# Rewriting an attention plus mixer kernel: full-array matmuls, activations kept in SBUF, 512-token MLP groups interleaved with attention, and crossbar transposes

## The chip, the cores and the metric

The kernel runs on one core of a Trainium2 chip. The metric is the device time of one launch in microseconds (us). Several executions were timed for each kernel; the text quotes medians. A run more than 1.5% above the fastest of its kernel counts as slow and stays out of the ratios.

Engine names in the profile: PE is TensorE (matmuls), PEld is the weight load of TensorE (it overlaps PE: in the kernel before the two are busy 442.4 and 746.2 us of a span of 883.4), DVE is VectorE, ACT is ScalarE, POOL is GpSimd, SP is SyncE. A "q" after a name (SPq) is the sequencer or queue of that engine. PEclk is the TensorE clock that was granted, as a share of full speed.

## The reference

The problem has 8 batches of 576 tokens. Attention has 8 heads of 64 channels, a band of 32 tokens to each side, and 8 global tokens. A mixer block follows it.

```python
# attention, per batch and head (q, k, v: 576 x 64)
scores = q @ k.T / sqrt(64)
mask   = |i - j| <= 32  or  i is global  or  j is global
attn   = softmax(where(mask, scores, -1e9));  x[:, head] = attn @ v
# mixer, per batch (x: 576 x 512)
tok = w_tok @ (alpha1 * x + beta1);     u = x + lam * tok          # token mix
ch  = relu((alpha2 * u + beta2) @ w_ch1) @ w_ch2                   # channel MLP, 512 -> 2048 -> 512
out = u + lam * ch
```

## The kernel before

The kernel before has two stages in sequence, and DRAM tiles between them. In the first stage each head loads q, k and v, transposes q and k on TensorE, and computes scores with operands of 64 rows. The product with V opens each of five output tiles with an 8-row matmul (the eight global keys) and adds two 128-row matmuls to it (one in the last tile).

```python
# stage 1, per batch and head (cut)
for c in range(NT):
    nc.tensor.transpose(out=trq[:, c, :], in_=qn16[:, c, :], identity=identb)        # L369
nc.vector.tensor_copy(out=QT, in_=trq)                                               # QT, KT: 64 rows
...
nc.tensor.matmul(out=scps[...], lhsT=KTf[:, c : c + P], rhs=QT[:, t, :], start=True, stop=True)           # L385, 64 rows
...
for t in range(NT):                                                                  # partB
    nc.tensor.matmul(out=pvps[...], lhsT=st["pgc"][:, gsl], rhs=st["vg_ext"], start=True, stop=False)     # L424, 8 rows
    for ci, bi in enumerate(tbis):
        nc.tensor.matmul(out=pvps[...], lhsT=PT[:, bi * P : (bi + 1) * P], rhs=rhs, start=False, ...)     # L429, 128 rows
...
nc.sync.dma_start(out=pxd.rearrange("(t p) f -> p t f", p=P), in_=prev["xstg"])      # x to DRAM
nc.gpsimd.indirect_dma_start(out=pxd, ..., in_=prev["xg"], compute_op=ALU.add)       # global rows added in DRAM
```

The token mix of batch b-1 is emitted in pieces among the heads of batch b. It reads x back from DRAM, and stores u to DRAM. The second stage reads u, transposes it on TensorE in fp32, and runs the MLP over 576 tokens in two halves of 288.

```python
# stage 2, per batch (cut)
nc.sync.dma_start(out=U, in_=u_dram[b])
for t in range(NT):
    for cc in range(4):
        nc.tensor.transpose(out=utps[:, cc, 0:tsz], in_=U[...], identity=ident[...])         # L504, fp32
    nc.vector.tensor_copy(out=UT[...], in_=utps[:, :, 0:tsz])                                # L505
for ec in range(16):
    for nn in range(2):                                                                      # 2 x 288 tokens
        ... 4 matmuls hps (L513), 1 Relu on ScalarE (L516)
for t in range(NT):                                                                          # 4 x 128 + 64 tokens
    ... 16 matmuls chps of 512 columns (L522), add U, store
```

The softmax here doesn't subtract the row's maximum and nothing guards it: scores larger than these inputs give would overflow.

## Time and profile before

| | before |
|---|---|
| time, median of the first 3 runs | 873.48 us (868.25 to 884.87) |
| TensorE recorded busy | 746.2 us, 84% |
| TensorE's share of the chain that ended last | 76% |
| set-up, with TensorE mostly idle | about 60 us |
| attention and token mix | about 468 us, 58 us per batch |
| hand-over through DRAM | about 30 us |
| channel MLP | about 330 us, 41 us per batch |

The profiled execution is the longest of the first three runs (span 883.4 us, device time 884.87), 1.9% above the fastest. The differences that the profile is read for are far larger than that. The lines below are from the page of the kernel before: busy time of each engine with its share of the span and its number of instructions, busy tenths and clock tenths in 40 equal slices (22 us each), and the chain that ended last.

```profile
PE 746.2 (84%) x5044; PEld 442.4 (50%) x5091; DVE 340.5 (39%) x865; ACT 326.1 (37%) x641; POOL 155.8 (18%) x295
...
PE   0158999998989989989999872989898989898998
...
PEclk9999999855656555556555575998998999899989
...
PE 76%; DVE 11%; DMA 7%; issue 3%; ACT 1%; SPq 0%; POOL 0%; POOLq 0%; DVEq 0%
```

TensorE is recorded as busy nearly everywhere after the set-up, and the chain lies mostly on it. The clock row shows that the busy share is not the whole story: between slice 9 and slice 24 the granted clock is about half, although TensorE is recorded as busy at 80% or more up to slice 23.

The next view is the table by windows for the kernel before. Its columns are the window, its length, then for each engine the busy us and the number of instructions, then the granted clock, the DMA share, and GB/s.

```profile
0.00:60.00 60.00, 11.91 (x98) 6.74 (x99) 29.93 (x103) 0.00 (x0) 1.37 (x7) 1.00 0.50 182
...
176.00:234.00 58.00, 52.99 (x395) 30.95 (x396) 32.01 (x86) 24.65 (x48) 19.39 (x36) 0.56 0.54 156
526.00:556.00 30.00, 9.17 (x42) 5.34 (x43) 11.25 (x12) 0.00 (x0) 1.46 (x1) 0.60 0.51 194
556.00:597.00 41.00, 38.13 (x228) 22.98 (x230) 7.38 (x12) 15.87 (x32) 0.00 (x0) 0.97 0.24 90
```

The four windows are the set-up, one batch of attention, the hand-over, and one batch of the MLP. The stages follow each other, so each has its own limit. TensorE has only 9 us of work in the 30 us of the hand-over.

Two stretches of TensorE's timeline show where its busy time goes. Columns: start, length, engine and line, operation with output and inputs, rows*columns of the array, shape, and number of matmuls in the group. A gap before the group and what ended it stand in square brackets.

```profile
103.50 0.23 PE L424 MATMUL pvps<-vg_ext,pgc 8*128 8x65 f16 x1
103.67 0.29 PE L429 MATMUL pvps<-vext,PT 128*128 128x65 f16 x2
103.89 0.23 PE L424 MATMUL pvps<-vg_ext,pgc 8*128 8x65 f16 x1
...
401.44 0.20 PE L424 MATMUL pvps<-vg_ext,pgc 8*128 8x65 f16 x1
401.58 0.23 PE L429 MATMUL pvps<-vext,PT 128*128 128x65 f16 x2
401.74 0.20 PE L424 MATMUL pvps<-vg_ext,pgc 8*128 8x65 f16 x1
...
619.24 14.11 PE L522 MATMUL chps<-W_199,HT 128*128 128x512 bf16 x63
...
634.72 0.66 PE L504 MATMUL utps<-ident,U 128*128 128x128 f32 x4 [0.90 <-DVE UT L505]
```

A tile of three 65-column matmuls, one with 8 rows and two with 128, takes 0.39 us at 103 us and 0.30 us at 401 us (start to start). A record is longer than the distance to the next start (0.23 us against about 0.06 us for two such matmuls of one mode), so lengths overlap; the distance between starts is what counts. In the MLP 63 matmuls of 512 columns take 14.1 us, so 0.22 us each. The MLP then stops for the fp32 transposes, with gaps of 0.8 to 0.9 us.

### The profile page before, as it was taken

The numbers are of one execution on the slowest core, as the hardware profiler recorded it, in microseconds if no ns is written. First come the engines' busy times: TensorE is split into PE (matmuls) and PEld (weight loads), VectorE is DVE, ScalarE is ACT, GpSimd is POOL, SyncE is SP. The second block draws the span as 40 slices with busy tenths as digits, with TensorE's granted clock in tenths as the row PEclk, the third lists the DMA queues.
The fourth block names the chain that finished last, engine by engine and source line by source line (L and its number), as shares of the span: only waits on it lengthen the run. The fifth ranks groups of instructions, "written<-read, shape, count | busy, mean of one in ns | idle before, by whom it ended". The sixth has DMA issues, their size and how long they took to land.

```text
span 883.4 us, 13205 instructions
## 1 busy us (share of the span) xinstructions
PE 746.2 (84%) x5044; PEld 442.4 (50%) x5091; DVE 340.5 (39%) x865; ACT 326.1 (37%) x641; POOL 155.8 (18%) x295
## 2 busy tenths in 40 slices
PE   0158999998989989989999872989898989898998
PEld 0026665564554654645545531646464645555564
DVE  2654446547465474474544734120202020211111
ACT  0005554443443433434524320616060624334251
POOL 0025433233242332313413200000000000000000
PEclk9999999855656555556555575998998999899989
DMA  4926464473652754636526425120302020202101
GB/s 121 374 53 161 115 179 131 146 205 77 204 162 75 216 159 141 191 85 198 160 72 191 130 108 192 61 95 18 114 13 102 15 100 36 78 36 78 49 6 54
DMA packets 116807, 103.81 MB, mean 118 GB/s; under 512 B 90504, under 2 KB 91032, under 8 KB 114184
## 3 DMA queue, kind: packets, MB, share of 16 engines
q1 hardware_dynamic: 108536, 83.57, 30.5%
q0 software_dynamic: 8208, 19.40, 7.2%
q8 instruction: 40, 0.66, 0.3%
q14 instruction: 23, 0.19, 0.1%
HBM read 72.23 MB, written 30.71 MB: 117 GB/s over the span
## 4 chain that ended last, share of the span: by engine, by line
PE 76%; DVE 11%; DMA 7%; issue 3%; ACT 1%; SPq 0%; POOL 0%; POOLq 0%; DVEq 0%
PE chps L522 15%; PE hps L513 15%; PE tkps L292 9%; PE scps L385 7%; PE pvps L429 7%; PE pvps L424 5%; PE trq L369 5%; PE scps L375 3%; PE pvps L406 3%; DMA w2raw<-in_moe_w_ch_dram 3%; DVE XL L282 2%; PE smp L438 2%; PE utps L504 2%; DVE X L278 2%; DVE UT L505 2%
## 5 line engine op out<-in xcount | busy, mean ns | idle before, releaser
L516 ACT ACTIVATE HT<-hps,bias1T 128x288 bf16<-128x288 f32 x256 | 127.2, 501 | 213.1 <-PE hps L513 212.6
L513 PE MATMUL hps<-UT,W_192 128*128 128x288 bf16 x1024 | 154.7, 293 | 1.6
L522 PE MATMUL chps<-W_199,HT 128*128 128x512 bf16 (+1 forms) x608 | 152.7, 381 | 2.9 <-ACT HT L516 1.3
L513 PEld LDWEIGHTS <-W_192 128*128 128x128 bf16 x1024 | 102.0, 100 | 48.3 <-issue 20.2
L526 DVE TENSOR_TENSOR ob<-chps,U 128x512 f32<-128x512 f32 (+1 forms) x40 | 27.6, 690 | 249.5 <-PE chps L522 249.5
L396 ACT ACTIVATE PT<-scps 128x1192 f16<-128x1192 f32 x64 | 74.5, 1164 | 109.3 <-PE scps L388 102.1
L292 PE MATMUL tkps<-XL,wtT 128*128 128x512 bf16 (+3 forms) x185 | 80.3, 555 | 19.4 <-DVE XL L282 15.6
L522 PEld LDWEIGHTS <-HT 128*128 128x128 bf16 (+1 forms) x640 | 62.4, 100 | 64.1 <-issue 3.4
L385 PE MATMUL scps<-QT,KT 64*128 64x128 bf16 x576 | 78.5, 283 | 7.6 <-DVE KT L376 7.6
L446 DVE COPY xstg<-pvps 128x320 f32<-128x320 f32 x64 | 31.4, 491 | 121.7 <-PE pvps L429 121.7
L424 PE MATMUL pvps<-vg_ext,pgc 8*128 8x65 f16 x320 | 72.0, 225 | 2.3 <-DVE vg_ext L411 2.0
L429 PE MATMUL pvps<-voext,PT 128*128 128x65 f16 x448 | 69.3, 234 | 0.0
L415 ACT ACTIVATE pgc<-pvps 8x640 f16<-8x640 f32 x64 | 44.3, 692 | 62.9 <-PE pvps L406 62.9
L306 POOL DMA_DIRECT2D vn<-in_v_dram x63 | 58.3, 926 | 49.5 <-ACT vext L357 38.7
L385 PEld LDWEIGHTS <-KT 64*128 64x128 bf16 x576 | 53.3, 125 | 21.8 <-DVE KT L376 11.4
L504 PE MATMUL utps<-ident,U 128*128 128x128 f32 (+1 forms) x160 | 29.6, 309 | 37.5 <-DVE X L278 19.5
L388 PE MATMUL scps<-qgT,KT 64*128 64x8 bf16 x320 | 61.1, 207 | 0.0
L351 POOL DMA_DIRECT2D vo<-in_v_dram x64 | 53.2, 831 | 11.7 <-ACT voext L360 9.3
L429 PEld LDWEIGHTS <-PT 128*128 128x128 f16 x576 | 39.9, 109 | 22.7 <-issue 3.8
L421 DVE TENSOR_TENSOR PT<-PT,mask 128x1192 f16<-128x1192 f16 x64 | 49.1, 768 | 2.6 <-ACT PT L396 2.2
L424 PEld LDWEIGHTS <-pgc 8*128 8x128 f16 x320 | 31.2, 98 | 33.4 <-issue 6.6
L292 PEld LDWEIGHTS <-wtT 128*128 128x128 bf16 (+3 forms) x200 | 21.4, 125 | 47.2 <-issue 42.6
(486 smaller groups left out, 834.4 us busy)
## 6 DMA issues: line engine op xcount, KB each, us to landing
qn<-in_q_dram SPq DMA_DIRECT2D x63, 160.0 KB, 2.6
kn<-in_k_dram SPq DMA_DIRECT2D x63, 160.0 KB, 3.3
vn<-in_v_dram POOLq DMA_DIRECT2D x63, 160.0 KB, 3.5
vo<-in_v_dram POOLq DMA_DIRECT2D x64, 128.0 KB, 3.3
out_dram<-ob SPq DMA_DIRECT2D x32, 256.0 KB, 2.0
w1raw<-in_moe_w_ch_dram SPq DMA_DIRECT2D x1, 4096.0 KB
w2raw<-in_moe_w_ch_dram SPq DMA_DIRECT2D x1, 4096.0 KB
xdram_60<-xstg SPq DMA_DIRECT2D x1, 1300.0 KB, 6.1
```

The costliest lines, as they stand in the source:

```text
L292: nc.tensor.matmul(out=tkps[0:tsz, :], lhsT=wtT[0:ssz, sc, t * P : t * P + tsz], rhs=st["XL"][0:ssz, sc, :], start=(sc == 0), stop=(sc == 4),)
L306: eng.dma_start(out=dst, in_=src_flat[bh * S : bh * S + SPAD, :].rearrange("(c p) d -> p c d", p=P))
L351: nc.gpsimd.dma_start(out=vo, in_=vf[bh * S + 64 : bh * S + S, :].rearrange("(c p) d -> p c d", p=P))
L385: nc.tensor.matmul(out=scps[:, bi * P : (bi + 1) * P], lhsT=KTf[:, c : c + P], rhs=QT[:, t, :], start=True, stop=True)
L388: nc.tensor.matmul(out=scps[:, GR_OFF + 8 * si : GR_OFF + 8 * si + 8], lhsT=KTf[:, c : c + P], rhs=g["qgT"][:, 8 * h : 8 * h + 8], start=True,
L396: nc.scalar.activation(out=PT, in_=scps[:, 0:SCORE_F], func=AF.Exp, bias=0.0, scale=0.125)
L421: nc.vector.tensor_tensor(out=PT, in0=PT, in1=mask, op=ALU.mult)
L424: nc.tensor.matmul(out=pvps[:, t * PV_T : t * PV_T + PV_T], lhsT=st["pgc"][:, gsl], rhs=st["vg_ext"], start=True, stop=False)
L429: nc.tensor.matmul(out=pvps[:, t * PV_T : t * PV_T + PV_T], lhsT=PT[:, bi * P : (bi + 1) * P], rhs=rhs, start=False, stop=(ci == len(tbis) ...
L513: nc.tensor.matmul(out=hps, lhsT=W1[:, cc, ec * P : (ec + 1) * P], rhs=UT[:, cc, tsl], start=(cc == 0), stop=(cc == 3))
L516: nc.scalar.activation(out=HT[:, ec, tsl], in_=hps, func=AF.Relu, bias=bias1T[:, ec : ec + 1], scale=1.0)
L522: nc.tensor.matmul(out=chps[0:tsz, :], lhsT=HT[:, ec, t * P : t * P + tsz], rhs=W2[:, ec, :], start=(ec == 0), stop=(ec == 15))
```

## The change

The intent is that TensorE should run one array mode, with large matmuls back to back, and that attention should hide among the matmuls of the MLP.

- Every matmul uses 128 rows and 128 columns, one small transpose in the set-up apart. Two heads share the 128 rows; q is laid out with zeros in the other head's rows. The 8 global keys of all heads share one 128-row operand (G and RG).
- x and u stay in SBUF. The DRAM round trips are gone.
- The MLP runs over nine flat groups of 512 tokens. The last 64 tokens of two batches make one shared tile ("S").
- q, k, u and w_tok are transposed by DMA through the crossbar (`dma_start_transpose`: the data are transposed on their way), apart from q and k of batch 0 and the gathered global rows.
- Attention and token mix of batch g+1 are placed between the 128 matmuls of group g, by a fixed program order; below this is called the weave.
- W2 is loaded and scaled during group 0.

```diff
 # cut to the core
-for c in range(NT):
-    nc.tensor.transpose(out=trq[:, c, :], in_=qn16[:, c, :], identity=identb)
+def xbar_k(b, c):
+    nc.sync.dma_start_transpose(out=KT[b % 2][:, :, 32 + c * P : 32 + (c + 1) * P], in_=Kb[:, c, :])
 ...
-nc.tensor.matmul(out=pvps[...], lhsT=st["pgc"][:, gsl], rhs=st["vg_ext"], start=True, stop=False)
+def pv_mms(b, hp, i, o):
+    mm(o, G[:, gs], RG[hp % 2], True, False)
+    for a in range(2):
+        mm(oa, pt[:, a, c0 : c0 + P], Ve[par][:, i, 2 * hp + a, :], False, i == 4)
 ...
-nc.sync.dma_start(out=u_dram[bb], in_=st["U"].rearrange("p t c -> p (t c)"))
+def finish_u(t, ps):
+    nc.vector.tensor_tensor(out=x, in0=ps, in1=x, op=ALU.add)
+    nc.gpsimd.tensor_tensor(out=ub, in0=x, in1=A2, op=ALU.mult)
+    nc.sync.dma_start_transpose(out=UT[g % 2][:, :, 128 * j : 128 * j + 128], in_=ub)
 ...
+def attention(b):          # scores s, products with V w, per pair of heads
+    ...
+            a += [s[0], w[0], s[1], w[1], w[2], s[2], w[3], w[4]]
+        if i < HP:
+            a.append(gq_pv(b, i))           # global queries; makes RG
 ...
+for w, f in token_mix(0):
+    f()
+...
+for f in xbars(1):         # ten q/k transposes of batch 1
+    f()
+for hp in range(HP):
+    qpad(hp)               # VectorE: QT -> QP, zero-padded
+gcols(1)                   # VectorE: KGP
+for g in range(9):
+    base = mlp(g)          # 64 matmuls of W1, 64 of W2, 512 columns each
+    if g == 0:
+        slots[0] += [lambda: w2_load(0), lambda: w2_load(1)]
+        ... w2_scale(blk) at slot 8 + 7 * blk
+    if nb < NB:            # nb = g + 2
+        timed(prefetch(nb), slots, 2, 60)
+        timed(xbars(nb), slots, 60, 100)
+        timed([... qpad ..., gcols(nb)], slots, 116, 127)
+    parts = [(attention(g + 1), 2, 90), (token_mix(g + 1), 94, 114)] if g + 1 < NB else []
+    weave(items, parts)
```

## The prediction

> **What bounds it now.** The chain of waits lies 76% on TensorE, 11% on VectorE, 7% on DMA. The table by windows shows serial stages:
> - set-up, about 60 us, TensorE busy 12 us;
> - attention plus token mixing, 60 to 528 us: a 58 us period per batch, TensorE recorded busy 53 of it, granted clock 0.50 to 0.59 from 176 us on;
> - after a 30 us hand-over, the channel MLP, about 41 us per batch at clock 0.93 to 1.0.
>
> Timeline: in MLP runs the 512-wide matmuls start 0.22 us apart, the 288-wide 0.122 us, so 80+128 need 33 us; the rest is mostly fp32 transposes of U (0.8 us gaps). In attention two same-mode 65-wide matmuls start 0.06 us apart, but a tile of one 8-row and two 128-row matmuls takes 0.30 to 0.39 us, not 0.18: up to 0.1 us per change of array mode. [...]
>
> **What the change does.** It removes all 64-row and 8-row modes, PE transposes of q, k and U after batch 0, the DRAM round trips of x and u, and ragged 576-token MLPs. Per batch, attention needs 36 score matmuls, 20 global, 92 PV (each near 0.062 us), 8 of 288 columns (0.122) and 25 token-mix of 512 (0.218): estimate 2.3+1.2+5.7+1.0+5.4 = 15.7 us. An MLP group of 128 matmuls of 512 columns: 27.9 us, nine of them.
>
> Estimate of the whole:
> - set-up and attention of batch 0, not overlapped (DMA, ACT and VectorE hops, token mixing, q/k crossbar transposes ahead of group 0): 70 us;
> - group 0, with W2 loaded and scaled underneath: 51 us;
> - groups 1 to 6: 43.6 us of matmuls each plus 3 us of stalls: 280 us;
> - groups 7, 8: 56 us; last stores 3 us.
>
> Sum 460 us. Other engines per 46 us group, from traced durations (ACT about 0.29 us + 0.73 ns per column; VectorE 0.69 us per 512 fp32 columns): ACT 19 us, VectorE 22 us; GpSimd an estimated 30 us (15 loads near 1 us, multiplies). So TensorE stays the bound, nearly all of the removed time was on the critical path, and attention under dense matmuls should keep the clock near 1.
>
> **Predicted: 460 us, 8 in 10 between 425 and 515. Faster 0.97, same 0.015, slower 0.015.**
>
> **What would show the steps.**
> - MLP matmuls 0.218 us apart, attention's 0.06 to 0.07, no mode gaps between; TensorE above 85% busy in groups.
> - Group 0 starting at 60 to 80 us; 44 to 48 us for groups 1 to 6, 28 us for 7 and 8.
> - Granted clock 0.9 or more from group 0 on.
> - Busy: ACT 150 to 190 us, VectorE 190 to 240 us.
>
> **What would make it wrong.**
> - Crossbar transposes: 14 or 15 of 128 KB per group on one in-order queue; the trace before has none. [...] at 1 to 1.5 us each they fit, at 4 us they would set the group (60 us) and give 560 us.
> - GpSimd: casting loads and multiplies in one queue; at 1.5 times my estimate it sets the group.
> - The clock falling to half in mixed groups: over 100 us.
> - A longer serial start: W1 and W_tok share the DMA with batches 0 and 1.
> - Tighter dependence of score, exp, mask, PV: 1 us per head pair is 28 us.

The 1 to 1.5 us and the 4 us for a crossbar transpose were estimates, since the trace before has none. So was the part of the multiplies in the 30 us for GpSimd; for the loads the trace before shows 0.83 to 0.98 us each.

## The result and the profile after

| | before | after |
|---|---|---|
| time, median of 4 runs | 879.17 us (868.25 to 892.9) | 496.74 us (495.06 to 497.37) |
| ratio of fast runs | | 0.567 (95% interval 0.563 to 0.5711) |
| HBM read / written | 72.23 / 30.71 MB | 39.38 / 9.44 MB |
| TensorE busy, matmuls | 746.2 us, x5044 | 387.7 us, x2727 |
| mean granted clock | 0.786 | 0.952 |

Ratios in this document are the mean time of one kernel's fast runs over that of the other's of the same rounds, so they are not quite the ratio of the medians that are quoted. The 0.567 comes out when the profiled run of the kernel before (884.87 us) is counted as fast; without it the ratio is 0.570. The outputs are right.

These are the lines of the page of the kernel after, in the order of those of before. A slice is 12.3 us here.

```profile
PE 387.7 (79%) x2727; PEld 204.8 (42%) x2727; DVE 241.4 (49%) x697; ACT 155.7 (32%) x275; POOL 218.8 (44%) x270
...
PE   0336640657897889978998898899889888999995
...
PEclk9998585687999999999999999999999999999999
...
PE 44%; DVE 23%; DMA 10%; issue 8%; SPq 5%; ACT 5%; POOL 3%; POOLq 0%; DVEq 0%; ACTq 0%
```

From slice 11 on the clock is full (1.00 from 123.3 us to the end), and until the last slice TensorE is busy for at least seven tenths. The first ten slices are different: TensorE is busy for 0 to 7 tenths, and the clock falls to half (0.50 between 50 and 60 us and between 74.3 and 89.1 us). VectorE's share of the chain has risen from 11% to 23%.

The same table by windows for the kernel after: set-up, group 0, group 1, group 2, group 7 and group 8. The borders are the starts of the first W1 matmul of each group, read from the timeline.

```profile
0.00:74.30 74.30, 30.20 (x298) 21.63 (x299) 44.45 (x133) 16.68 (x33) 41.14 (x54) 0.88 1.16 155
74.30:150.40 76.10, 49.69 (x317) 25.03 (x318) 41.44 (x108) 17.01 (x30) 32.41 (x40) 0.80 0.85 131
150.40:195.00 44.60, 40.70 (x304) 21.59 (x304) 22.85 (x69) 16.66 (x30) 22.89 (x30) 1.00 1.07 117
195.00:244.50 49.50, 43.65 (x317) 22.89 (x318) 27.04 (x82) 16.68 (x30) 30.02 (x36) 1.00 1.00 109
432.80:460.50 27.70, 27.70 (x130) 12.57 (x129) 2.77 (x4) 10.99 (x16) 0.00 (x0) 1.00 0.15 51
460.50:493.30 32.80, 27.74 (x129) 12.38 (x127) 3.46 (x5) 10.99 (x16) 0.00 (x0) 1.00 0.12 40
```

Groups start at 74.3, 150.4, 195.0, 244.5, 289.9, 339.3, 384.9, 432.8 and 460.5 us. Groups 1 to 6 take 282.5 us together, 44.6 to 49.5 us each; the longer ones carry six token-mix tiles and the shorter ones four. In groups 1 and 2 TensorE idles 4 to 6 us. Group 0 takes 76 us for the same matmuls, and TensorE is idle for 26 of them. Its busy time is longer too: 49.7 us against 43.7 us in group 2, which has as many matmuls on record (317). At the clock of 0.80 the matmuls themselves cost about 6 us more, an estimate from these two lines.

The timeline of TensorE in the kernel after, inside group 0 at a clock of 1.00 (97 to 100 us), answers to the two stretches of before:

```profile
98.43 0.22 PE L119 MATMUL bank<-RG,G 128*128 128x130 f16 x1
98.49 0.19 PE L119 MATMUL bank<-Ve,PT 128*128 128x65 f16 x1
98.52 0.19 PE L119 MATMUL bank<-Vo,PT 128*128 128x65 f16 x1
98.55 0.19 PE L119 MATMUL bank<-Ve,PT 128*128 128x65 f16 x1
98.58 0.20 PE L119 MATMUL bank<-Vo,PT 128*128 128x65 f16 x1
98.61 0.81 PE L119 MATMUL bank<-UT,W 128*128 128x512 bf16 x3
```

A tile of V products for two heads, five matmuls, now takes 0.18 us from start to start; before, the tiles of two heads took 0.60 to 0.78 us. The 65-column matmuls start 0.03 us apart. No gap separates attention from the MLP.

The waits of TensorE in the kernel after (total us, times, longest us):

```profile
PE bank L119 <- DVE RG L310: 32.7, 25, 3.3
PE bank L119 <- DVE KGP L222: 17.9, 6, 13.8
PE bank L576 <- DVE UT L570: 17.5, 3, 10.9
PE bank L119 <- DMA UT<-UB: 7.6, 2, 7.4
```

RG and KGP are operands for the global tokens, UT is u transposed (in the set-up, at L570 and L576, the same tile holds q and k of batch 0).

The second line holds one wait of 13.8 us. It stands at the start of group 0, and the queue of SyncE shows where it comes from:

```profile
64.24 6.33 SPq L403 DMA_TRANSPOSE UT<-UB  x4
70.61 1.26 SPq L208 DMA_TRANSPOSE KT<-Kb  x1
71.92 1.26 SPq L211 DMA_TRANSPOSE QT<-Qb  x1
...
82.57 1.22 SPq L211 DMA_TRANSPOSE QT<-Qb  x1
83.97 0.46 SPq L204 DMA_DIRECT2D Vo<-Ve  x1
```

The ten crossbar transposes of q and k of batch 1 are queued behind the four transposes of u, which come out of the token mix of batch 0. Each holds the queue for about 1.25 us, against 0.46 us for a plain copy. They end at 84 us. VectorE then copies QT into QP (85.17 us) and KGP after that, and the first attention matmul of group 0 starts at 89.11 us.

### The profile page after: what moved, and what is told of

It reads as the page before. It is cut to its first block, busy times and chain, and to the rows that moved or that the text cites. A ratio compares the mean times of both kernels' runs of the same rounds, so it can differ in the third digit from the quotient of the medians.

```text
span 493.3 us, 7444 instructions
## 1 busy us (share of the span) xinstructions
PE 387.7 (79%) x2727; PEld 204.8 (42%) x2727; DVE 241.4 (49%) x697; ACT 155.7 (32%) x275; POOL 218.8 (44%) x270
## 3 DMA queue, kind: packets, MB, share of 16 engines
HBM read 39.38 MB, written 9.44 MB: 99 GB/s over the span
## 4 chain that ended last, share of the span: by engine, by line
PE 44%; DVE 23%; DMA 10%; issue 8%; SPq 5%; ACT 5%; POOL 3%; POOLq 0%; DVEq 0%; ACTq 0%
PE bank L119 43%; DVE PT L292 4%; DVE QP L216 4%; ACT E L280 3%; DVE PGQ L287 3%; DMA UT<-UB 3%; DMA KG<-in_k_dram,hidx 2%; DVE RG L310 2%; SPq L208 2%; SPq L211 2%; DVE XR L338 2%; DVE RGt L309 2%; DMA XR<-in_moe_w_ch_dram 1%; DVE SR L338 1%; POOL UB L401 1%
## 5 line engine op out<-in xcount | busy, mean ns | idle before, releaser
L119 PE MATMUL bank<-UT,W 128*128 128x512 bf16 x576 | 160.7, 387 | 9.2 <-DMA UT<-UB 7.6
L119 PE MATMUL bank<-W,HT 128*128 128x512 bf16 x576 | 142.5, 379 | 0.0
L470 ACT ACTIVATE HT<-bank,bias 128x512 bf16<-128x512 f32 x144 | 98.9, 687 | 85.3 <-PE bank L119 82.5
L119 PEld LDWEIGHTS <-HT 128*128 128x128 bf16 x576 | 52.0, 98 | 50.6
L401 POOL TENSOR_TENSOR UB<-XR,A 128x512 bf16<-128x512 f32 x32 | 40.5, 1267 | 58.9 <-DMA UT<-UB 25.8
L119 PEld LDWEIGHTS <-W 128*128 128x128 bf16 x640 | 50.8, 99 | 35.9 <-issue 11.0
L119 PE MATMUL bank<-RG,G 128*128 128x130 f16 x160 | 36.0, 226 | 32.7 <-DVE RG L310 32.7
L280 ACT ACTIVATE E<-bank 128x416 f16<-128x416 f32 (+1 forms) x96 | 48.0, 511 | 40.5 <-PE bank L119 40.3
L483 DVE TENSOR_TENSOR XR<-bank,XR 128x512 f32<-128x512 f32 x32 | 21.9, 685 | 54.9 <-PE bank L119 54.9
L119 PE MATMUL bank<-XL,wtT 128*128 128x512 bf16 x180 | 44.9, 379 | 0.8 <-ACT wt4o L688 0.8
L119 PE MATMUL bank<-Ve,PT 128*128 128x65 f16 x320 | 40.6, 199 | 0.0
L398 DVE TENSOR_TENSOR XR<-bank,XR 128x512 f32<-128x512 f32 x32 | 22.1, 691 | 36.1 <-PE bank L119 36.1
L216 DVE COPY QP<-QT 64x576 bf16<-64x576 bf16 x56 | 25.0, 446 | 18.7 <-DMA QT<-Qb 18.1
```

The lines of the kernel that those rows point to most:

```text
L119: nc.tensor.matmul(out=o, lhsT=l, rhs=r, start=st, stop=sp, skip_group_check=True)
L216: nc.vector.tensor_copy(out=QP[r, hp, a, :, 0:64], in_=QT[r, hp, 0:S].rearrange("p (t j) -> p t j", j=64))
L280: nc.scalar.activation(out=e[:, UOFF[u] : UOFF[u + 1]], in_=ps[:, 0:off], func=AF.Exp, bias=0.0, scale=0.125)
L398: nc.vector.tensor_tensor(out=x, in0=ps, in1=x, op=ALU.add)
L401: nc.gpsimd.tensor_tensor(out=ub, in0=x, in1=A2, op=ALU.mult)
L470: nc.scalar.activation(out=HT[:, ec, :], in_=st["ps"], func=AF.Relu, bias=bias1[:, ec : ec + 1], scale=1.0)
```

## The experiments

The theory was: the change gains from full-row matmuls and from the weave, TensorE is the bound from group 1 on, and the excess over the predicted time is a start-up chain. Each expectation names its own theories A and B. Row padding was tested in the kernel before; the other experiments change the kernel after. Except for e5 to e8, for which the medians alone are quoted, a ratio to the kernel before of the same rounds is given. e1 computes something else, as told there. In these rounds the kernel before had medians of 879.6 to 881.1 us, with fast runs averaging about 876 us.

### e2_before_gpv128: only the 8-row matmuls of the kernel before padded to 128 rows

```diff
-vg_ext = pA.tile([8, PV_T], FP16, name="vg_ext")
+vg_ext = VGX[h % 2]        # persistent [128, 65] tile, zeroed once; rows 0 to 7 written
-pgc = pA.tile([8, SPAD], FP16, name="pgc")
+pgc = PGC[h % 2]           # persistent [128, 640] tile, zeroed once
```

> The kernel before, with one thing changed: the 8-row matmul of the global keys (5 per head) gets zero-padded 128-row operands, so within PV the array mode no longer changes. Same number of matmuls and columns, same result. Theory A (a change of array mode costs 0.06 to 0.1 us, on the critical path): 10 changes per head x 64 heads x 0.08 us = 51 us less: about 825 us (810 to 845), the tile of three matmuls at about 0.1 to 0.18 us instead of 0.30 to 0.39. Theory B (small matmuls cost the same in any mode, or the attention stage is bound by its dependences): within 1% of before.

Measured: 807.7 us (807.5 to 809.7), ratio 0.9224 (0.914 to 0.9308). The timeline of this kernel at the same place and at matmuls of the same record length (0.20 us):

```profile
406.61 0.20 PE L424 MATMUL pvps<-vgx,pgcx 128*128 128x65 f16 x1
406.65 0.23 PE L429 MATMUL pvps<-vext,PT 128*128 128x65 f16 x2
406.71 0.19 PE L424 MATMUL pvps<-vgx,pgcx 128*128 128x65 f16 x1
406.75 0.22 PE L429 MATMUL pvps<-voext,PT 128*128 128x65 f16 x2
```

The tile falls from 0.30 to 0.10 us with the same number of matmuls and the same columns, so each of its two changes of mode cost about 0.1 us. The padding removes nine changes per head (ten, less the one from scores to V products, which stays), 576 in all. The fast means differ by 68 us, 0.118 us per change; some of that may be the clock, whose mean rose from 0.79 to 0.85. Theory A holds, and the gain is a little larger than expected.

### e5_before_row128: in addition, the 64-row operands of the scores padded to 128 rows

```diff
-QT = pA.tile([64, NT, P], BF16, name="QT")
-KT = pA.tile([64, NT, P], BF16, name="KT")
+QT, KT = QTX[h % 2], KTX[h % 2]          # persistent [128, 5, 128], rows 64 to 127 zero; qgT and kgT too
```

> e2 once more with the score and global-score operands zero-padded to 128 rows as well, so that of the row modes only the fp32 transposes of 64 rows are left; same matmuls, same result. e2 measured 0.107 us per removed change (69 us over 640). Theory A (every change costs that on the critical path): about 4 more changes per head, 256 in all, 27 us: about 782 us (770 to 792). Theory B (after e2 the attention stage is no longer bound by TensorE): 800 us or more.

Measured: 780.44 us (779.9 to 783.8), mean clock 0.907. This is inside A's range. Row modes alone, in the old program, are worth about 95 us (fast means 876 over all rounds, 874 in this one, to 781). The old program with full rows is still 284 us slower than the new one, so the modes are a quarter of the gain, not most of it.

### e1_block: the new kernel without the weave

```diff
-parts = [(attention(g + 1), 2, 90), (token_mix(g + 1), 94, 114)] if g + 1 < NB else []
+parts = [(attention(g + 1) + token_mix(g + 1), 2, 2)] if g + 1 < NB else []
```

The same instructions run, but attention and token mix of batch g+1 stand in one block after the second MLP matmul of group g.

> The changed kernel, but in each of the first seven groups the attention and token mix of the next batch are emitted as one block at the group's third matmul instead of being spread between matmuls 2 and 114. Same instructions, same result. Theory A (the weave is a main part of the gain: the score, exp, mask, PV chain has to hide under dense matmuls): batch 0, which runs unwoven in the set-up, needs about 28 us for work whose matmuls take 13; 7 groups x about 14 us: 590 us (560 to 620), TensorE waiting mainly for ACT E and VectorE PGQ and RG, and a granted clock below 0.9 in the blocks. Theory B (the gain is the smaller number of matmuls and the single array mode; order matters little): below 515 us.

Measured: 668.69 us (664.6 to 673.7), ratio 0.7633 (0.7539 to 0.7727), mean clock 0.795. That is 172 us more than the kernel after, and beyond A's range. But not all of it is the weave. Two windows of this kernel, the MLP of one group and then the block:

```profile
290.00:318.00 28.00, 27.14 (x123) 12.16 (x124) 4.68 (x11) 10.30 (x15) 7.23 (x9) 0.98 1.22 122
318.00:361.00 43.00, 23.09 (x179) 15.72 (x179) 22.01 (x68) 6.96 (x14) 16.46 (x21) 0.62 0.21 38
```

The MLP alone takes 28 us at a clock of 0.98. The block takes 43 us: TensorE is idle 20 us of it (6.8 us on UT, 4.9 us on RG, 4.8 us on PGQ, the rest on others) and the granted clock is 0.62. The wait on UT stands at the end of the block. This is the end of the block on TensorE's timeline:

```profile
347.47 6.58 PE L119 MATMUL bank<-XL,wtT 128*128 128x512 bf16 x18 [0.22 <-issue]
360.90 16.18 PE L119 MATMUL bank<-UT,W 128*128 128x512 bf16 x61 [6.85 <-DMA UT<-UB]
```

And this is the line of UT in the waits of the whole run:

```profile
PE bank L119 <- DMA UT<-UB: 58.0, 8, 8.5
```

In the kernel after that line has 7.6 us in 2 waits. The edit of e1 made the rest. There are two tiles UT, and group g reads UT[g % 2]. Some tiles of batch g+1 belong to group g+2, so the token mix of that batch writes into the tile that group g reads. In the kernel after this happens at matmuls 94 to 114, when the 64 W1 matmuls that read it are done. In e1 it happens ahead of 62 of them: they wait for the transposes, and they read the u of other tokens. So e1 does not compute the same result, against what its expectation says. The check did not see it: in the reference, lam is drawn with a standard deviation of 0.01, and the term of the MLP is about 1% of the output (root mean squares, computed from its inputs). Seven of the eight waits stand behind the seven blocks and sum to 50 us. Without them e1 would take about 619 us, the upper end of A's range, and the weave would be worth about 120 us. Both are estimates, and no run without the fault was made.

Inside the block the 65-column matmuls start 0.055 to 0.06 us apart (clock 0.62); in the woven kernel it is 0.03 (at 98 us, clock 1.00). So an attention block loses twice: each VectorE or ScalarE result that TensorE waits for is bare, and the clock falls, which slows the matmuls as well. What pulls it down is not shown: the block has waits (20 of 43 us) and, between 318.6 and 346.7 us, no 512-column matmuls, but in the kernel before the clock was 0.56 with TensorE recorded busy for 53 of 58 us. In the block the pace of 0.06 us is there at 326 us, within 8 us of the last 512-column matmul and with no idle gap above 1.6 us in between. This also bears on a point of the prediction: the 0.06 us that was read in the kernel before is the pace of this block, not that of the woven kernel. The first tile of e2 at 102 us shows 0.055 us too, with records of 0.25 us.

### e4_xbar_early: q/k transposes of batch 1 ahead of the token mix of batch 0

```diff
+for f in xbars(1):
+    f()
 for w, f in token_mix(0):
     f()
 ...
-for f in xbars(1):
-    f()
```

> The changed kernel with the q/k crossbar transposes of batch 1 issued before token mix of batch 0 instead of after it; nothing else moved. Theory A (the 13.8 us TensorE wait at the start of group 0 is only the place of these ten transposes in the queue; their inputs landed by 52 us): 482 us (478 to 487). Theory B (the DMA queues are the limit there, so the wait only moves to another place): 492 us or more.

Measured: 482.93 us (480.6 to 484.6), ratio 0.5502 (0.5447 to 0.5556). The longest wait on KGP falls from 13.8 to 1.1 us:

```profile
PE bank L119 <- DVE KGP L222: 4.0, 5, 1.1
```

The wait was real and on the critical path: its whole length came back. Group 0 still takes 65 us (74.2 to 139.3), so this is not its only excess.

### e3_xbar_twice and e6_xbar_scratch: more crossbar transposes

These two ask whether the crossbar queue is close to setting the period of a group. In e3 each q/k transpose is issued twice to the same place:

```diff
+for _ in range(2):
     a.append(lambda c=c: xbar_k(b, c))
     a.append(lambda c=c: xbar_q(b, c))
```

> The changed kernel with every crossbar transpose of q and k from batch 1 on issued twice in a row (same destination, same result): 10 more per batch, 12.5 us more of issue on the sync queue at the 1.25 us each that the trace shows. Theory A (the crossbar is off the critical path in the woven groups, on it only ahead of group 0): about +12.5 us, all between token mix of batch 0 and group 0, so 510 us (503 to 520). Theory B (the crossbar queue is close to setting the group): +12.5 us in each of 7 groups, about 590 us.

Measured: 551.53 us (550.6 to 552.1), ratio 0.6291. It fits neither number, and the experiment was flawed: the second transpose of each pair waits until the first has landed (between 130 and 450 us the queue waits 44.3 us on KT and 9.9 us on QT), a cost that the change under study does not have. In e6 the extra ten go to four scratch tiles instead:

```diff
 a.append(lambda c=c: xbar_k(b, c))
+a.append(lambda c=c: xbar_s(Kb[:, c, :]))      # scratch destination, four in turn
 a.append(lambda c=c: xbar_q(b, c))
+a.append(lambda c=c: xbar_s(Qb[:, c, :]))
```

> e3 repeated without its flaw: in e3 the second transpose of a pair waited for the first to land, because both wrote the same bytes. Here the ten extra q/k transposes per batch write four scratch tiles in turn. Right result. Theory A (the crossbar queue has slack in the woven groups): +12.5 us ahead of group 0 only, 510 us (503 to 520). Theory B (the queue is near its limit, so added issue time delays the transposes of U that the next group waits for): over 530 us.

Measured: 545.9 us (543.3 to 548.1). Theory A, that the queue has room, misses by 36 us. Group 0 rises from 76 to 99 us: the added transposes stand in the chain that e4 showed to be critical, and the wait on KGP grows from 13.8 to 25.4 us. Groups 1 to 6 rise from 282.5 to 313 us, about 5 us each. The queue of SyncE in e6, in one of these groups:

```profile
246.43 1.21 SPq L219 DMA_TRANSPOSE QT<-Qb  x1
261.18 1.16 SPq L494 DMA_DIRECT2D out_dram<-SR  x2
262.39 1.28 SPq L216 DMA_TRANSPOSE XS<-Qb  x1
...
279.36 6.48 SPq L411 DMA_TRANSPOSE UT<-UB  x3
```

The queue issues nothing from 247.6 to 261.2 us. It runs in program order, and the next entry is the store of the first output tile, whose data are ready only when TensorE has done the 80th matmul of the group. Nine of the twenty transposes of q and k stand behind that store in the program order, and ahead of or among the transposes of u, which the next group needs first. So the queue is not full; what is behind the store comes too late. This is a hypothesis at this point, and e12 tests it.

### e12_xbar_spread: e6 with most of the transposes moved ahead of the store

```diff
-timed(xbars(nb), slots, 60, 100)
+timed(xbars(nb), slots, 20, 90)
```

> e6 (ten extra q/k transposes per batch into scratch) with the transposes of a group spread over matmuls 20 to 90 instead of 60 to 100. In e6 the sync queue stood idle for 13 us in front of the first output store (matmul 79), with transposes queued behind it, which then ran into those of U. Theory A (the queue has room; what hurts is the place behind the waiting stores): groups 1 to 6 back to 46 to 48 us, total about 518 us (510 to 526), the rest being the extra 12 us ahead of group 0 and some in it. Theory B (the added transposes cost time wherever they stand, by load on the DMA engines): 538 us or more.

Measured: 511.61 us (507.2 to 515.7), ratio 0.5838; inside A's range; its profiled run counts as slow, so only the spans of groups and the waits are read from it. Groups 1 to 6 take about 284 us again, as in the kernel after with half as many transposes, and the waits on UT fall from 30.7 to 7.2 us. Group 0 is still long (94 us, KGP wait 25.5 us), since nothing was moved there. So the queue has room for twenty transposes of 1.25 us per group on top of those of u. Where they stand in its order decides.

### e7_rg_slack: e4 with one score step moved ahead of the V products

After each pair of heads, RG is made by three VectorE operations and the first V product needs it. The line at the top of the waits (32.7 us in 25 waits) is that dependence.

```diff
-a += [s[0], w[0], s[1], w[1], w[2], s[2], w[3], w[4]]
+a += [s[0], s[1], w[0], w[1], s[2], w[2], w[3], w[4]]
```

> e4 with one change of order in the woven attention: both first score units of the next head pair go ahead of the first PV tile (s0 s1 w0 w1 s2 w2 w3 w4 instead of s0 w0 s1 w1 w2 s2 w3 w4). Theory A (the 34 us that TensorE waits for RG is too little distance between the global-query PV and the first PV tile): about 0.7 us more distance per head pair, 468 us (462 to 475), the RG waits at most half. Theory B (VectorE's own order sets RG, so the wait moves along): 479 us or more.

Measured: 472.0 us (470.5 to 473.1), 11 us less than e4. Waits on RG fall from 34.3 to 18.7 us, in 12 waits instead of 25, a little more than the half that A named. Many of the stalls in the groups come from too little distance between a VectorE result and its first use in the program order, and moving one unit of work between them recovers between 1.5 and 2 us in each of the seven groups.

### e8_w2_direct: e4 with W2 loaded straight into its bf16 tile in the set-up

```diff
+for blk in range(8):        # after prefetch(1)
+    nc.gpsimd.dma_start(out=W2[:, 2 * blk : 2 * blk + 2, :], in_=w_ch2[...])     # casting load
-            ... in0=W2S[blk % 2][:, i, :], in1=LAM ...                            # fp32 staging, load chained to scale
+            ... in0=W2[:, 2 * blk + i, :], in1=LAM ...                            # scaled in place, same slots
```

> e4 with W2 loaded by casting DMAs straight into its bf16 tile during the set-up and scaled in place in the same slots of group 0 (rounded twice, so a slightly larger error); no staging, no load that waits for a scale. Theory A (group 0 takes 65 us against 47 to 49 of its successors because W2 scaling waits for its loads in VectorE's queue and attention waits behind it): group 0 near 52 us, total 470 us (464 to 476). Theory B (group 0 is slow for the clock and the gathers): 479 us or more.

Measured: 486.23 us (484.7 to 488.6), no gain. Group 0 shrank from 65 to 58 us, so W2's staging did hold VectorE's in-order queue. But group 0 started at 81.9 us in place of 74.2, behind a wait of 15.2 us on the transposes of u: the four took a median of 8.4 us to land (2.3 us in e4 at the same place) while the 4 MB of W2 moved, and the second pair waited for the buffers of the first. So transposes issued by SyncE took more than three times as long to land while loads issued by GpSimd moved.

### e10_setup and e11_w2_late: the set-up again

e10 is e7 with the gather of the global rows ahead of the loads of V, and the cast and transposes of the second pair of heads ahead of what needs the gather:

```diff
-load_v(0, 1)
-load_v(0, 2)
 ...
 gather(0)
+load_v(0, 1)
+load_v(0, 2)
 ...
-gather_tr(0)
-gcols(0)
 b0_cast(1)
 b0_tr(1)
+gather_tr(0)
+gcols(0)
```

> e7 with the set-up reordered: the gather of the global keys and queries is issued ahead of the first two v loads (it took 9.9 us to land behind them against 4 us later), and VectorE's cast of head pair 1 no longer stands behind the products that wait for that gather. Theory A (TensorE's 11 us wait for UT in the set-up is this one gather at the head of VectorE's queue, and all of batch 0 follows): 4 to 7 us less, 466 us (463 to 469). Theory B (ACT work and the loads of q, k set the start): 470 us or more.

Measured: 473.2 us (471.4 to 474.3), ratio 0.5409, no gain on e7. The gather landed in 4.8 us instead of 9.4 us in the kernel after, which has e7's order there (means of two), the scores of the first pair of heads started 2 us sooner (20.7 for 22.6 us), and the token mix of batch 0 still started at 60.2 us (60.1 in e7). The saved wait turned up again ahead of the later pairs of heads, where ScalarE and VectorE copy the transposed q and k out of PSUM. So the gather does not bind the set-up. That this chain does is read from the waits and was not tested.

e11 is e10 with the direct loads of W2 issued after the token mix of batch 0, and its scaling at slots 20 + 5 * blk instead of 8 + 7 * blk.

> e10 with W2 loaded by casting DMAs straight into place (as in e8) but issued after token mix of batch 0, not before, and scaled in place a little later in group 0. In e8 group 0 shrank from 65 to 58 us but started 8 us later, because the W2 traffic was ahead of the transposes of U. Theory A (order on the DMA engines was the cause): the 7 us are kept, about 459 us (456 to 463), group 0 starting as in e10. Theory B (W2 costs that time wherever it is put): within 3 us of e10.

Measured: 467.62 us (467.4 to 467.8), ratio 0.5351 (0.5297 to 0.5404). It lies between the two theories, 5.6 us under e10 and 8.6 us above A's value. Group 0 starts at 75.97 us, as in e10 (76.02), and takes 59.1 us instead of 63.6. The clock in group 0 is 0.91, where the kernel after had 0.80. This is the fastest version, 6% below the kernel after and clear of both kernels.

## Why the prediction was right, and where it was off

The prediction was 460 us with a range of 425 to 515; the result is 496.74 us, faster by far and inside the range, 37 us above the centre.

**The bound and the stages were read correctly.** The pieces that the prediction wanted removed were on the critical path, and the time fell by nearly as much as computed. Going from before to after through e5 and e1, with means of fast runs: 876 us, 781 with full rows, 669 without the weave (about 619 when the 50 us that e1's edit added are taken off), 497 with the weave. So about 95 us belong to array modes, about 160 us to the rest (no DRAM hand-over, 512-token groups, fewer matmuls, no TensorE transposes; not separated further here), and about 120 us to the weave. The last two are estimates, and the shares depend on the order of the steps.

**Array modes: right.** The prediction said "up to 0.1 us per change"; e2 measured about 0.10 us in the timeline, and 0.118 us by total time.

**Groups 1 to 6: right as a sum, with two errors that cancel in part.** 280 us were predicted and 282.5 measured. The V products were costed at 0.062 us, the pace of the kernel before, which e1 has at a clock of 0.62; in the new kernel, at 1.00, 65-column matmuls start 0.03 us apart. So the matmuls of a group take less than 43.6 us, and stalls more than the 3 us allowed: TensorE idles 3.9 us in group 1 and 5.9 us in group 2. e7 shows that about 2 us per group are the wait on RG.

**Groups 7 and 8 and the tail: right.** 56 us were predicted for the two groups; 27.7 us for group 7 and 27.7 us of matmuls in group 8 give 55.4 us. The tail is 5 us instead of 3.

**Clock: right from group 1 on, wrong in group 0. Other engines: right.** The prediction expected 0.9 or more from group 0 on. Group 0 had 0.80, with a TensorE that was 65% busy where above 85% was expected. The clock row shows nine tenths or more from group 1 on, and 1.00 in the four windows shown. ScalarE is busy 155.7 us (150 to 190 predicted), and VectorE 241.4 us, just above the range of 190 to 240.

**Group 0: the term that was mis-sized.** The prediction put the set-up at 70 us and group 0 at 51. The set-up took 74.3 us and group 0 took 76.1. These two terms hold 29 us of the 37. The rest is 2.5 us in groups 1 to 6, about 2 us in the tail, and 3.4 us between the span of the profiled run and the median device time, which the sum left out. Three parts of group 0 are identified:

- 13.8 us is the wait for the q/k transposes of batch 1. The prediction counted them in the set-up, "ahead of group 0". In the program order they stand behind the transposes of u in the same queue, so they ran after the first matmuls of group 0 were ready. e4 removes the wait and gains 14 us.
- 4.5 to 7 us is W2: VectorE waits for the next block of W2 while results for attention stand behind it in program order (3.3 us in one such wait in e4). e8 and e11 show group 0 shorter by 7 and 4.5 us when W2 does not pass through the staging tiles.
- The rest is not settled by a run. e11 still has 59 us in group 0, against 43 to 48 in its groups 1 to 6. Its timeline shows one wait of 5.3 us there on KGx (the gathered rows of batch 2), smaller ones on RG and PGQ, and a mean clock of 0.91. No experiment takes these apart. The slower matmuls of group 0 (about 6 us, see above) are spread over all three parts.

**Crossbar transposes: the cost was right, the criterion was not.** The prediction asked whether one takes 1 to 1.5 us or 4, both estimates. It is 1.25 us, and groups are not bound by them. But e6 added ten per group at that cost and lost about 5 us per group, and e12 took the loss away without removing one. The condition that matters is what each stands behind in the in-order queue, which a sum of durations does not show.

**The weave: not in the sum.** The prediction summed matmul times, which does not say what the same matmuls would take in another order. The first estimate of that, in e1's expectation, was 590 us (560 to 620); e1 took 669, or about 619 without its fault. The prediction also named a fall of the clock in mixed groups as a risk. The clock does fall in unmixed attention blocks (0.62 in e1). Of the mixed groups it falls only in group 0 (0.80): it is 0.50 from 74.3 to 89.1 us, which holds the wait of 13.8 us, and 0.59 between 110 and 120 us; from 150.4 us to the end it is 1.00.

Still open: how the 160 us divide, what the weave is worth in a run without e1's fault, what pulls the clock down, the last 11 us of group 0, and why the granted clock is recorded as 1.00 in the kernel before around 103 us, where the 65-column matmuls keep the 0.06 us that e1's block has at 0.62.

## What to carry to other kernels

Place latency-bound stages (scores, exp, mask, small products) between the matmuls of a dense stage by program order: it hides their waits, and here the clock was 1.00 in the woven groups 1 and 2 against 0.62 in e1's block. When engines and queues run in order, check for each queue what an instruction stands behind, above all in the first iteration, where loads, set-up and steady-state work share the queues; a budget of busy times does not find these waits (13.8 us at the start of group 0, about 5 us per group in e6). When an experiment moves work, check which buffers it now writes before they have been read: e1 carried 50 us of waits that its own edit had made. Pad small operands to the full array before anything else: at 0.1 us per change of mode it gave 11% in the old program for a few lines of zeros.
